# Block attention and a mixture of experts on one core: score products from plain float32 K and Q on row halves, in place of float32r parts

## The chip, the core and the metric

The kernel runs on one core of a Trainium2 chip. The metric is device time in microseconds. Three runs of the kernel before took 888.95 us in the median (888.78 to 889.32).

## What is computed

Four batches, eight heads, 576 positions, head dimension 64. Each head's scores are masked by blocks of 64 positions (a query sees its own block and all before it); the attention output becomes 2304 rows of 512, and four experts with weights per row follow.

```python
scores = scale * np.matmul(q, k.transpose(0, 1, 3, 2))
mask = block_i >= block_j                 # block_i = pos // 64
attn = softmax(np.where(mask, scores, -1e9))
x = (attn @ v).transpose(0, 2, 1, 3).reshape(2304, 512)
p = domain_probs / domain_probs.sum(-1)
out = sum(p[:, e] * (relu(x @ w1[e]) @ w2[e]) for e in range(4))
```

## The kernel before, in words

The rows are worked in five blocks (`BLOCKS`, line 21): the first holds the first 64 positions of all four batches (256 rows), the other four hold positions 64 to 575 of one batch each (512 rows). The experts' part goes over the blocks in chunks of 128 hidden columns: `mm1` (line 1106) makes 12 matmuls a chunk (three products of high and low float32r parts by four slices of the 512 inputs), `relu` splits the result again, and `mm2` (line 1148) adds into four PSUM accumulators. Blocks 0 to 2 take 96 chunks; blocks 3 and 4 are done together at the end by `both_blocks` (line 1291), from sums of their inputs that `prepare` (line 1223) makes once all attention is over.

Attention of the four 512-row blocks is made of 16 units, one for a batch and a pair of heads (`unit`, line 435). `PLAN` (line 26) puts the units of batch b in phase b + 1. A unit runs as several threads:

- `k_thread` and `q_thread` load K and Q in 32-column strips and transpose them on vector, so that the head dimension lies on partitions: kT has one head on partitions 0 to 63 and the other on 64 to 127.
- `v_thread` loads V into VN.
- `s_thread` makes the scores: the keys are cut in pieces of 128 (for 512 queries that see ever more keys, pieces of 512, 448, 320, 192 columns, and one of 64 for the odd block), and pieces of up to 512 columns share a PSUM bank. `mask` writes a large negative number where a piece covers keys that a query may not see.
- `e_thread` copies the banks to S in SBUF and takes the running maximum over pieces in cm.
- `m_thread` takes the maximum over partitions on GpSimd, then vector subtracts it and scalar takes the exponential.
- `pv_flow` (line 774) multiplies by V. In phases 2 to 4 two units go together (`mates`), and both S buffers are free only after that.

There are two ways to make the scores. Phase 1 (`plain`, line 439) takes float32 kT and qT as they are: head 0 on partitions 0 to 63 and head 1 on 64 to 127, one matmul for each head and piece (line 567), with two banks for a group of pieces, one for each head; the order of pieces and the place of the odd piece come from `pieces_beside` (line 284). It draws its banks from the two att banks and two accumulator banks that are not in use yet. Phases 2 to 4 split K and Q into a high part, which is a cast to float32r, and a low part, which is the rest: KK holds K's high part on 64 partitions and its low part on the other 64, HH holds Q's high part on both halves, LL its low part, and two matmuls over 128 partitions (lines 579 and 580) make one piece of one head. The odd piece of both heads is made together (lines 628 and 629), with the two unwanted quarters masked. Their banks are the two att banks alone.

The order of the instructions is made in the program by a planner (`Flow`, line 81). Each thread yields operations with an engine and a cost; at each step `run` (line 198) takes the one that can start first, by priority among those that are near, and puts it on its engine's queue. Units start to load when the chunk number reaches `GATES` (line 37). `late` adds distance between a matmul and its inputs in the plan: 800 ns for scores in phase 1 and 3000 ns in phases 2 to 4 (lines 46 and 47), and half of that after a bank's last use. Loads go from SP's queue.

Of the kernel before, what the change touches and what calls it, by code (L numbers as in the profile page):

```python
# [17 lines left out]
PEO = 13.5  # L18
# [230 lines left out]
def kernel(  # L249
# [78 lines left out]
    for tag, n, shape, dt in (  # L328
        ("kr", 2, [P, S], F32),
        ("qr", 1, [P, 2 * MAXW], F32),  # L330
        ("kT", 1, [P, S], F32),
        ("qT", 1, [P, 2 * MAXW], F32),
        ("KK", 2, [P, 2 * S], F32R),
        ("HH", 1, [P, 2 * MAXW], F32R),
        ("LL", 1, [P, 2 * MAXW], F32R),
        ("VN", 2, [P, (MASK_BLOCK + MAXW) // P + 1, 3, D], F32),
        ("tr", 1, [P, MAXW], F32),
        ("tc", 1, [P, MAXW // 8], F32),
        ("S", 2, [P, 2 * MAXC], F32),
        ("cm", 1, [P, 2 * MAXW], F32),  # L340
        ("mx", 1, [P, 2 * MAXW], F32),
        ("sa", 1, [P, 2 * MAXW], F32),
        ("sb", 1, [P, 2 * MAXW], F32),
        ("xs", 2, [P, MAXW], F32),
        ("rc", 1, [P, MAXW], F32),
    ):
        bufs(tag, n, shape, dt, attn)
        counts[tag] = n
# [19 lines left out]
    def late(o, by):  # L368


        o.lag = by
        return o
# [62 lines left out]
    def unit(u, ua, us, ju, pu, ph, job, dst, c):  # L435
# [5 lines left out]
        pcs, C = pieces_beside(q0, q1) if plain else pieces_of(q0, q1)  # L441
# [6 lines left out]
        def k_thread():  # L448
# [16 lines left out]
            if plain:  # L465
                st["k"] = (kT, [t], [t])
                return
            KK = yield fl.take("KK", us)
            kt, kk = kT.tile, KK.tile
            a1 = yield a_copy(kk[0:64, :q1], kt[0:64, :q1], q1, [t], [kT, KK], pr)  # L470
            l1 = yield tt(BOTH, kk[64:128, :q1], kt[0:64, :q1], kk[0:64, :q1], SUB, q1, [a1], [kT, KK], pr)
            rot = MASK_BLOCK * odd
            second = []
            for to, of, n in ((q1 + rot, 0, q1 - rot), (q1, q1 - rot, rot)):
                if n:
                    second.append((yield a_copy(kk[64:128, to:to + n], kt[64:128, of:of + n], n, [t], [kT, KK], pr)))
                    second.append((yield tt(BOTH, kk[0:64, to:to + n], kt[64:128, of:of + n], kk[64:128, to:to + n],
                                            SUB, n, second[-1:], [kT, KK], pr)))
            fl.give(kT)
            st["k"] = (KK, [a1, l1], second)  # L480

        def q_thread():
# [4 lines left out]
            for h, j in ((h, j) for h in range(2) for j in range(2 if plain else 4)):  # L487
                p0, c0 = (64 * h + 32 * j, 0) if plain else (32 * j, h * W)
                vals.append((yield dma(
                    qr.tile[p0:p0 + 32, c0:c0 + W].rearrange("c (i r) -> c i r", r=32),  # L490
                    q[b, h0 + h, q0:q1, 32 * (j % 2):32 * (j % 2) + 32].rearrange("(i c) r -> c i r", c=32),
                    W * 128, u=[qr], prio=pr, packet=128)))
            yield ("until", lambda: left_first[0] == 0 and past["w"] > 2)
            qT = yield fl.take("qT", ua)
            n = W if plain else 2 * W
            t = yield op("dve", 1.04 * n + 70, lambda _: nc.vector.transpose(out=qT.tile[:, :n], in_=qr.tile[:, :n]),
                         vals, [qr, qT], pr)
            fl.give(qr)
            if plain:
                st["q"] = (qT, t)  # L500
                return
# [4 lines left out]
            fl.give(qT)  # L506
            st["q"] = (HH, LL, a, l)

        def v_thread():
# [11 lines left out]

        def mask(r, o, m, pb):

            def fn(e):
                if e == "act":
                    nc.scalar.activation(o, ident[r:r + 64, :64], AF.Copy, bias=neg, scale=0.0)
                else:
                    nc.vector.memset(o, neg)

            return op([("act", 193.0), ("dve", 120.0)], 0, fn, [m], [pb], pr - 1.0)  # L530

        banks = []
        for h in range(2):
            cur, used = [], 0
            for pc in pcs:
                if pc[0] is None and not plain:
                    continue
# [7 lines left out]
        if plain:  # L545
            banks.sort(key=lambda x: (x[1][0][0], x[0]))
        elif odd:
            banks.append((None, [pcs[-1]]))

        def s_thread():  # L550
# [6 lines left out]
            KK, ka, kb = st["k"]  # L557
            lag = LAG_FIRST if plain else LAG
            if plain:
                qT, qv = st["q"]  # L560
                Q = [qT]
                need = lambda h: ka + [qv]
                cost = lambda w: 2 * max(107.0, 2 * w / 2.4 + 2.5)

                def product(o, h, k0, n, lo):
                    hp = slice(64 * h, 64 * h + 64)
                    nc.tensor.matmul(out=o, lhsT=KK.tile[hp, k0:k0 + n], rhs=qT.tile[hp, lo:W], start=True, stop=True)  # L567
            else:
                HH, LL, qa, ql = st["q"]
                Q = [HH, LL]  # L570
                Hv = HH.tile[:, :2 * W].rearrange("p (h w) -> p h w", h=2)
                Lv = LL.tile[:, :2 * W].rearrange("p (h w) -> p h w", h=2)
                need = lambda h: (ka + kb if h is None else kb if h else ka) + [qa, ql]
                cost = lambda w: 2 * max(85.0, w / 2.4 + PEO)

                def product(o, h, k0, n, lo):
                    at = k0 + (q1 + MASK_BLOCK * odd) * h
                    hs = h
                    nc.tensor.matmul(out=o, lhsT=KK.tile[:, at:at + n], rhs=Hv[:, hs, lo:W], start=True, stop=False)  # L579
                    nc.tensor.matmul(out=o, lhsT=KK.tile[:, at:at + n], rhs=Lv[:, hs, lo:W], start=False, stop=True)  # L580

            for h, ps_list in banks:
                if plain:

                    if h:
                        continue
                    two = []
                    for _ in range(2):
                        two.append((yield fl.take("att", None, bank_tag)))

                    def fn(_, two=two, ps_list=ps_list):
                        at = 0
                        for j, a, w, _ in ps_list:
                            for g in range(2):
                                product(two[g].tile[:, at:at + w], g, q1 - P if j is None else P * j, P, a - q0)
                            at += w

                    ws = [x[2] for x in ps_list]
                    m = yield late(op("pe", 300.0 + (2 * sum(ws) + ws[0] - sum(abs(x - y) for x, y in zip(ws, ws[1:]))) / 1.2,
                                 fn, need(0), [*two, KK] + Q, pr), lag)  # L600
                    for g in range(2):
                        done, at, spots = [m], 0, {}
                        for j, a, w, _ in ps_list:
                            r = 64 if j is None else 128 if a == P * j else None
                            if r:
                                spots.setdefault(r, []).append(at)
                            at += w
                        for r, x in spots.items():
                            o = two[g].tile[r - 64:r, x[0]:x[0] + 64]
                            if len(x) == 2:  # L610
                                o = two[g].tile[r - 64:r, x[0]:2 * x[1] - x[0]].rearrange("p (n w) -> p n w", n=2)[:, :, :64]
                            i = ident[r - 64:r, :64 * len(x)]
                            i = i.rearrange("p (n w) -> p n w", n=2) if len(x) == 2 else i
                            done.append((yield op("act", 0.833 * 64 * len(x) + 140, lambda _, o=o, i=i: nc.scalar.activation(
                                o, i, AF.Copy, bias=neg, scale=0.0), [m], [two[g]], pr)))
                        st["banks"].append((g, ps_list, two[g], done))
                    continue
                pb = yield fl.take("att", None, bank_tag)
                ps = pb.tile
                use = [pb, KK] + Q  # L620
                done = []
                if h is None:
                    lo = W - MASK_BLOCK
# [887 lines left out]
```

## Time and profile before

| | |
|---|---|
| median of three runs | 888.95 us |
| span of the profiled execution | 887.2 us |
| TensorE busy | 879.6 us, 99% |
| VectorE busy | 694.1 us, 78% |
| ScalarE busy | 464.9 us, 52% |
| GpSimd busy | 139.8 us, 16% |
| hardware DMA queue q1 | 38.5% of 16 engines |

Of the profiled execution its span is known, from its first to its last instruction; the time of a run has in addition what lies before and after. Matmuls are pipelined and their ends are modelled, so the duration of one is not its cost: the distance from one start to the next is. A float32 matmul has two records, since it is issued in two parts.

### The profile page before, as it was taken

To read this page: it belongs to the slowest core of one execution; us is meant where nothing else is said; L and a number is where in the kernel's file an instruction comes from. 1 tells how busy PE (TensorE), PEld (TensorE's weight loads), DVE (VectorE), ACT (ScalarE), POOL (GpSimd) and SP (SyncE) were. 2 spreads that over 40 slices of the span, in tenths; PEclk is the share of its full clock that TensorE was granted. 3 is DMA by queue.
4 is the path that set the end of the run, shared out by engine and by line. 5 is a ranking of instruction groups with operands and counts; after the bars stand their busy time and mean duration, and the time that the engine had idled before them with its cause. 6 is when DMAs were issued, how large, how long until landed. Compare 5 with 4: busy or idle time off the path is not lost.

```text
span 887.2 us, 12597 instructions
## 1 busy us (share of the span) xinstructions
PE 879.6 (99%) x4403; PEld 712.6 (80%) x4403; DVE 694.1 (78%) x1205; ACT 464.9 (52%) x968; POOL 139.8 (16%) x53
## 2 busy tenths in 40 slices
PE   8999999999999999999999999999999999999998
PEld 6777788878878877877878878888888888888887
DVE  6899999899898898898998789965565655666532
ACT  6796766765755664656754644544343333333220
POOL 1141100422314312412412430000000000000000
PEclk9999999999999999999999999999999999999999
DMA  7877458545455355456434222312021112110002
GB/s 170 218 182 210 131 135 200 152 140 124 97 133 128 79 133 124 127 137 158 91 92 122 83 84 84 120 48 71 24 76 40 62 47 61 48 48 24 13 1 95
DMA packets 212879, 91.18 MB, mean 103 GB/s; under 512 B 126416, under 2 KB 194256, under 8 KB 212816
## 3 DMA queue, kind: packets, MB, share of 16 engines
q1 hardware_dynamic: 211808, 89.86, 38.5%
q8 instruction: 34, 0.56, 0.3%
q10 hardware_dynamic: 1008, 0.52, 0.2%
q14 instruction: 29, 0.24, 0.1%
HBM read 85.63 MB, written 4.72 MB: 102 GB/s over the span
## 4 chain that ended last, share of the span: by engine, by line
PE 94%; DMA 2%; SPq 2%; ACT 1%; DVE 1%; issue 0%; DVEq 0%
PE acc L1171 24%; PE h L1120 24%; PE acc L1417 20%; PE h L1352 10%; PE att L1352 7%; PE att L805 5%; PE att L580 2%; SPq L380 2%; PE att L579 2%; DMA probs_n<-in_moe_domain_probs_dram 1%; DMA w2r<-in_moe_w_dram 1%; PE acc L567 0%; DMA w1r<-in_moe_w_dram 0%; PE acc L805 0%; DMA S<-in_k_dram 0%
## 5 line engine op out<-in xcount | busy, mean ns | idle before, releaser
L1120 PE MATMUL h<-xh,w1h 128*128 128x512 f32 (+1 forms) x384 | 137.0, 357 | 0.0
L1120 PE MATMUL h<-xh,w1l 128*128 128x512 f32 (+1 forms) x384 | 136.0, 354 | 0.0
L1120 PE MATMUL h<-xl,w1h 128*128 128x512 f32 (+1 forms) x384 | 135.9, 354 | 0.0
L1171 PE MATMUL acc<-w2h,hh 128*128 128x512 f32 x312 | 124.0, 398 | 0.0
L1171 PE MATMUL acc<-w2h,hl 128*128 128x512 f32 x312 | 121.8, 390 | 0.6 <-DVE hl L1140 0.6
L1171 PE MATMUL acc<-w2l,hh 128*128 128x512 f32 x312 | 121.8, 390 | 0.0
L730 POOL PARTITION_ALL_REDUCE sb<-sa x26 | 84.0, 3279 | 170.8 <-DVE tr L845 99.7
L389 ACT CAST w2h<-w2r 128x512 fp32r<-128x512 f32 x113 | 70.2, 621 | 70.6 <-PE acc L1171 57.2
L396 DVE TENSOR_TENSOR w1l<-w1r,w1h 128x512 fp32r<-128x512 f32 (+1 forms) x128 | 88.3, 692 | 3.4 <-ACT w1h L389 2.2
L751 POOL PARTITION_ALL_REDUCE mx<-cm x16 | 52.8, 3299 | 222.4 <-DVE cm L396 174.9
L396 DVE TENSOR_TENSOR w2l<-w2r,w2h 128x512 fp32r<-128x512 f32 x116 | 81.0, 699 | 5.3 <-ACT w2h L389 5.1
L1138 ACT ACTIVATE hh<-h 128x512 fp32r<-128x512 f32 (+1 forms) x94 | 49.3, 524 | 66.0 <-PE h L1120 64.9
L389 ACT CAST w1h<-w1r 128x512 fp32r<-128x512 f32 (+1 forms) x109 | 66.5, 611 | 29.1 <-DMA w1r<-in_moe_w_dram 12.4
L1120 PEld LDWEIGHTS h<-xh,w1h 128*128 128x128 f32 x384 | 72.5, 189 | 11.4 <-issue 0.9
L1120 PEld LDWEIGHTS h<-xl,w1h 128*128 128x128 f32 x384 | 72.5, 189 | 10.3
L1120 PEld LDWEIGHTS h<-xh,w1l 128*128 128x128 f32 x384 | 72.4, 189 | 10.2
L1171 PEld LDWEIGHTS acc<-w2h,hl 128*128 128x128 f32 x312 | 58.6, 188 | 13.8 <-DVE hl L1140 1.1
L1171 PEld LDWEIGHTS acc<-w2h,hh 128*128 128x128 f32 x312 | 58.7, 188 | 13.5 <-issue 1.2
L1171 PEld LDWEIGHTS acc<-w2l,hh 128*128 128x128 f32 x312 | 58.8, 188 | 9.9
L1140 DVE SCALAR_TENSOR_TENSOR hl<-h,hh 128x512 fp32r<-128x512 f32 (+1 forms) x94 | 55.4, 589 | 13.4 <-ACT hh L1138 12.9
L396 DVE TENSOR_TENSOR S<-S,mx 128x1024 f32<-128x1024 f32 (+4 forms) x80 | 59.6, 788 | 1.2 <-POOL mx L751 1.1
L707 ACT ACTIVATE S<-S 128x1024 f32<-128x1024 f32 (+4 forms) x80 | 55.4, 714 | 4.3 <-DVE S L396 4.0
(335 smaller groups left out, 1816.6 us busy)
## 6 DMA issues: line engine op xcount, KB each, us to landing
w2r<-in_moe_w_dram SPq DMA_DIRECT2D x128, 256.0 KB, 2.9
w1r<-in_moe_w_dram SPq DMA_DIRECT2D x120, 256.0 KB, 3.0
qr<-in_q_dram SPq DMA_DIRECT2D x112, 64.0 KB, 2.3
kr<-in_k_dram SPq DMA_DIRECT2D x64, 72.0 KB, 2.9
VN<-in_v_dram SPq DMA_DIRECT2D x32, 128.0 KB, 2.8
out_dram<-o SPq DMA_DIRECT2D x11, 256.0 KB, 2.6
w1rp<-in_moe_w_dram SPq DMA_DIRECT2D x8, 256.0 KB, 2.8
out_dram<-op SPq DMA_DIRECT2D x4, 256.0 KB, 2.1
```

The lines of the kernel that those rows point to most:

```text
L389: o = op(engs, 0, lambda e: nc.scalar.copy(dst, src) if e == "act" else nc.vector.tensor_copy(dst, src), r, u, prio)
L396: o = op(engs, 0, lambda e: ENG[e].tensor_tensor(out=dst, in0=a, in1=b, op=alu), r, u, prio)
L707: exps.append((yield op("act", 0.833 * 2 * w + 95, lambda _: nc.scalar.activation(sv, sv, AF.Exp, scale=scale), [t], [Sb], pr)))
L730: sums.append((yield held(2300.0, op("pool", 150 + 6.3 * W, lambda _, h=h: nc.gpsimd.partition_all_reduce(sb.tile[:, h * W:h * W + W], sa. ...
L751: lambda _: nc.gpsimd.partition_all_reduce(mx.tile[:, :2 * W], src, P, RED.max),
L805: nc.tensor.matmul(out=x.tile[64 * g:64 * g + 64, W - w:W], lhsT=lhsT, rhs=rhs, start=(i == 0), stop=(i == len(todo) - 1))
L1120: nc.tensor.matmul(out=ps[:, :n], lhsT=s.tile[:, ks], rhs=x.tile[:, kc, :n], start=(kc == 0 and m == 0), stop=(kc == KC - 1 and m == 2),)
L1138: a = yield op("act", 0.833 * n + 55, lambda _: nc.scalar.activation(hh.tile[:, :n], ps[:, :n], AF.Relu), [mm], [pb, hh], 0.0)
L1140: l = yield op("dve", 1.04 * n + 70, lambda _: nc.vector.scalar_tensor_tensor(out=hl.tile[:, :n], in0=ps[:, :n], scalar=0.0, in1=hh.tile[: ...
L1171: nc.tensor.matmul(out=acc, lhsT=s.tile[:, ts], rhs=w.tile, start=(f == 0 and m == 0), stop=(f == FC - 1 and m == 2))
L1352: nc.tensor.matmul(out=ps[:, :n], lhsT=w.tile[:, ks], rhs=x[:, kc, :n], start=(start and kc == 0 and m == 0), stop=(i in (2, 3, 4) and kc ...
L1417: nc.tensor.matmul(out=acc[:, to], lhsT=s.tile[:, ts], rhs=w.tile[:, to], start=(c == 0 and x == 0), stop=(c == 3 and x == 2), skip_group_ ...
```

## The change

All 16 units make their scores in the way of phase 1. K and Q are no longer split: KK, HH and LL are gone, kT and qT have two buffers, Q is loaded once for each head, the order of pieces is that of `pieces_beside`, and the odd piece of each head stands in a bank with others and takes the last 128 keys, of which the first 64 are masked. So VN holds the last 128 rows of V for each head, in place of 64 rows of both. The masks of a group are written by scalar, one for all pieces of a bank that need the same rows. A group takes two banks at once. The distance in the plan (`lag`), the banks that phases 2 to 4 may use and the pairing of units in `pv_flow` stay.

```diff
@@ pools
-        ("qr", 1, [P, 2 * MAXW], F32),
-        ("kT", 1, [P, S], F32),
-        ("qT", 1, [P, 2 * MAXW], F32),
-        ("KK", 2, [P, 2 * S], F32R),
-        ("HH", 1, [P, 2 * MAXW], F32R),
-        ("LL", 1, [P, 2 * MAXW], F32R),
+        ("qr", 1, [P, MAXW], F32),
+        ("kT", 2, [P, S], F32),
+        ("qT", 2, [P, MAXW], F32),
@@ unit
-        pcs, C = pieces_beside(q0, q1) if plain else pieces_of(q0, q1)
+        pcs, C = pieces_beside(q0, q1)
@@ k_thread
-            if plain:
-                st["k"] = (kT, [t], [t])
-                return
-            KK = yield fl.take("KK", us)
-            kt, kk = kT.tile, KK.tile
-            a1 = yield a_copy(kk[0:64, :q1], kt[0:64, :q1], q1, [t], [kT, KK], pr)
-            l1 = yield tt(BOTH, kk[64:128, :q1], kt[0:64, :q1], kk[0:64, :q1], SUB, q1, [a1], [kT, KK], pr)
...
+            st["k"] = (kT, [t])
@@ q_thread
-            for h, j in ((h, j) for h in range(2) for j in range(2 if plain else 4)):
-                p0, c0 = (64 * h + 32 * j, 0) if plain else (32 * j, h * W)
+            for h, j in ((h, j) for h in range(2) for j in range(2)):
+                p0 = 64 * h + 32 * j
...
-            HH = yield fl.take("HH", us)
-            LL = yield fl.take("LL", us)
-            a = yield a_copy(HH.tile[:, :2 * W], qT.tile[:, :2 * W], 2 * W, [t], [qT, HH], pr)
-            l = yield tt(BOTH, LL.tile[:, :2 * W], qT.tile[:, :2 * W], HH.tile[:, :2 * W], SUB, 2 * W, [a], [qT, HH, LL], pr)
...
+            st["q"] = (qT, t)
@@ v_thread
-                r, o, n = (slice(0, P), 2 * h, P) if plain else (slice(64 * h, 64 * h + 64), 1, MASK_BLOCK)
-                jv.append((yield dma(VJ.tile[r, at, o, :], v[b, h0 + h, q1 - n:q1], n * 256, u=[VJ], prio=pr + 0.005, packet=256)))
+                n = P
+                jv.append((yield dma(VJ.tile[:, at, 2 * h, :], v[b, h0 + h, q1 - n:q1], n * 256, u=[VJ], prio=pr + 0.005, packet=256)))
@@ s_thread
-                    nc.tensor.matmul(out=o, lhsT=KK.tile[:, at:at + n], rhs=Hv[:, hs, lo:W], start=True, stop=False)
-                    nc.tensor.matmul(out=o, lhsT=KK.tile[:, at:at + n], rhs=Lv[:, hs, lo:W], start=False, stop=True)
...
+            def product(o, h, k0, n, lo):
+                hp = slice(64 * h, 64 * h + 64)
+                nc.tensor.matmul(out=o, lhsT=KK.tile[hp, k0:k0 + n], rhs=qT.tile[hp, lo:W], start=True, stop=True)
...
+                two = []
+                for _ in range(2):
+                    two.append((yield fl.take("att", None, bank_tag)))
...
+                        for g in range(2):
+                            product(two[g].tile[:, at:at + w], g, q1 - P if j is None else P * j, P, a - q0)
...
@@ pv_flow
-                                    lhsT = VJ.tile[:, j, 2 * g, :] if j is not None else VJ.tile[:, nj, 2 * g if plain else 1, :]
+                                    lhsT = VJ.tile[:, j, 2 * g, :] if j is not None else VJ.tile[:, nj, 2 * g, :]
```

## Rows read from the trace of the kernel before

**Rows 1.** The page's first line.
```profile
span 887.2 us, 12597 instructions
```
**Rows 2.** Busy time by stretch: stretch, length, engines' busy (count), granted clock, DMA share, GB/s.
```profile
0.00:50.00 50.00, 45.96 (x401) 34.74 (x401) 39.74 (x99) 34.33 (x103) 7.11 (x13) 1.00 0.78 191
...
130.00:550.00 420.00, 420.00 (x2013) 338.06 (x2010) 375.84 (x618) 248.81 (x527) 117.36 (x36) 1.00 0.47 120
```
**Rows 3.** Waits of PE: who waited for whom, us in total, times, longest.
```profile
PE att L567 <- ACT cm L683: 1.5, 2, 0.9
...
PE acc L985 <- DVE st L978: 0.2, 1, 0.2
```
**Rows 4.** The chain that ended last: start, length, engine and line, count.
```profile
137.81 2.72 PE h L1120 x12
...
462.62 5.33 PE att L805 x40
...
525.97 5.33 PE att L805 x40
```
**Rows 5.** Timeline of PE, one unit of phase 2: start, length, instruction.
```profile
202.36 0.39 PE L579 MATMUL att<-HH,KK 128*128 128x512 f32 x1
...
203.22 0.39 PE L1120 MATMUL h<-xh,w1h 128*128 128x512 f32 x1
...
205.95 0.30 PE L579 MATMUL att<-HH,KK 128*128 128x320 f32 x1
...
206.44 0.41 PE L1171 MATMUL acc<-w2h,hh 128*128 128x512 f32 x1
206.70 0.39 PE L1171 MATMUL acc<-w2l,hh 128*128 128x512 f32 x1
...
218.11 0.22 PE L628 MATMUL att<-HH,KK 128*128 128x128 f32 x1
...
218.28 0.45 PE L1120 MATMUL h<-xh,w1h 128*128 128x512 f32 x1
218.56 0.39 PE L1120 MATMUL h<-xl,w1h 128*128 128x512 f32 x1
```
**Rows 6.** Timeline of PE in phase 1, groups of two units.
```profile
61.40 0.39 PE L1171 MATMUL acc<-w2h,hl 128*128 128x512 f32 x1
61.72 1.13 PE L567 MATMUL acc<-qT,kT 64*128 64x192 f32 x8
62.78 0.50 PE L1171 MATMUL acc<-w2h,hh 128*128 128x512 f32 x1
63.12 0.40 PE L1171 MATMUL acc<-w2l,hh 128*128 128x512 f32 x1
...
83.38 0.40 PE L1171 MATMUL acc<-w2h,hl 128*128 128x512 f32 x1
83.70 1.13 PE L567 MATMUL acc<-qT,kT 64*128 64x512 f32 x4
84.66 1.09 PE L567 MATMUL att<-qT,kT 64*128 64x448 f32 x8
85.68 0.50 PE L1171 MATMUL acc<-w2h,hh 128*128 128x512 f32 x1
```
**Rows 7.** Groups by line and form, VectorE: count, busy us, mean ns, idle before.
```profile
L396 DVE TENSOR_TENSOR LL<-qT,HH 128x1024 fp32r<-128x1024 f32 x12 | 19.0, 1580 | 0.2
...
L396 DVE TENSOR_TENSOR KK<-kT,KK 64x576 fp32r<-64x576 f32 x12 | 10.8, 897 | 1.1 <-ACT KK L389 0.7
```
**Rows 8.** The same view, ScalarE: emptying and masking of score banks.
```profile
L683 ACT COPY S<-att 128x512 f32<-128x512 f32 x56 | 32.7, 583 | 4.3 <-PE att L580 3.8
...
L526 ACT ACTIVATE att<-ident 64x64 f32<-64x64 f32 x90 | 20.0, 223 | 20.4 <-PE att L629 6.8 <-PE att L580 6.1 <-DVE probs_n L1444 1.9
```
**Rows 9.** Tile S3h: durations min/median/max, first and last start.
```profile
L1352 PE MATMUL h<-S3h,w1hp x8: 389/389/389, 555.2 to 789.1; 128*128 128x512 f32 x8
...
L396 DVE TENSOR_TENSOR S3l<-xr,S3h x1: 1217/1217/1217, 547.5 to 547.5; 128x1024 fp32r<-128x1024 f32 x1
```

More of the change, by code (lines that the diff above doesn't have):

```diff
@@ L494, in q_thread @@
             qT = yield fl.take("qT", ua)
-            n = W if plain else 2 * W
-            t = yield op("dve", 1.04 * n + 70, lambda _: nc.vector.transpose(out=qT.tile[:, :n], in_=qr.tile[:, :n]),
+            t = yield op("dve", 1.04 * W + 70, lambda _: nc.vector.transpose(out=qT.tile[:, :W], in_=qr.tile[:, :W]),
                          vals, [qr, qT], pr)
             fl.give(qr)
-            if plain:
-                st["q"] = (qT, t)
-                return
-            HH = yield fl.take("HH", us)
-            LL = yield fl.take("LL", us)
-            a = yield a_copy(HH.tile[:, :2 * W], qT.tile[:, :2 * W], 2 * W, [t], [qT, HH], pr)
-            l = yield tt(BOTH, LL.tile[:, :2 * W], qT.tile[:, :2 * W], HH.tile[:, :2 * W], SUB, 2 * W, [a], [qT, HH, LL], pr)
-            fl.give(qT)
-            st["q"] = (HH, LL, a, l)
+            st["q"] = (qT, t)
         def v_thread():
@@ L520, in v_thread @@
             st["v"] = (VJ, jv)
[L522 to L530, printed above, removed]
         banks = []
@@ L535, in unit @@
             for pc in pcs:
-                if pc[0] is None and not plain:
-                    continue
                 if used + pc[2] > 512:
@@ L544, in unit @@
                 banks.append((h, cur))
[L545 to L548, printed above, removed]
+        banks.sort(key=lambda x: (x[1][0][0], x[0]))
         def s_thread():
@@ L556, in s_thread @@
             st["banks"] = []
-            KK, ka, kb = st["k"]
+            KK, ka = st["k"]
             lag = LAG_FIRST if plain else LAG
[L559 to L578, printed above, removed]
-                    nc.tensor.matmul(out=o, lhsT=KK.tile[:, at:at + n], rhs=Hv[:, hs, lo:W], start=True, stop=False)
-                    nc.tensor.matmul(out=o, lhsT=KK.tile[:, at:at + n], rhs=Lv[:, hs, lo:W], start=False, stop=True)
@@ L582, in s_thread @@
-            for h, ps_list in banks:
[L583 to L616, printed above, removed]
-                    continue
[L618 to L623, printed above, removed]
-                    n = 2 * MASK_BLOCK
-                    def fn(_, ps=ps, n=n, lo=lo):
-                        lhsT = KK.tile[:, q1 - MASK_BLOCK:q1 + MASK_BLOCK]
-                        nc.tensor.matmul(out=ps[:, :n], lhsT=lhsT, rhs=Hv[:, :, lo:W], start=True, stop=False)
-                        nc.tensor.matmul(out=ps[:, :n], lhsT=lhsT, rhs=Lv[:, :, lo:W], start=False, stop=True)
-                    m = yield late(op("pe", 220.0, fn, need(None), use, pr), lag)
-                    m1 = yield mask(64, ps[64:128, 0:64], m, pb)
-                    m2 = yield mask(0, ps[0:64, 64:128], m, pb)
-                    done = [m, m1, m2]
-                else:
@@ new lines, in s_thread, with fn @@
+            qT, qv = st["q"]
+            def product(o, h, k0, n, lo):
+                hp = slice(64 * h, 64 * h + 64)
+                nc.tensor.matmul(out=o, lhsT=KK.tile[hp, k0:k0 + n], rhs=qT.tile[hp, lo:W], start=True, stop=True)
+            for h, ps_list in banks:
+                if h:
+                    continue
+                two = []
+                for _ in range(2):
+                    two.append((yield fl.take("att", None, bank_tag)))
+                def fn(_, two=two, ps_list=ps_list):
@@ L636, in s_thread @@
                     at = 0
-                    corners = []
                     for j, a, w, _ in ps_list:
-                        def fn(_, o=ps[:, at:at + w], j=j, h=h, a=a):
-                            product(o, h, P * j, P, a - q0)
-                        m = yield late(op("pe", cost(w), fn, need(h), use, pr), lag)
-                        done = [m]
-                        if a == P * j:
-                            corners.append(at)
-                        at += w
-                    for x in corners:
-                        done.append((yield mask(64, ps[64:128, x:x + 64], done[0], pb)))
@@ L650, in s_thread @@
-                st["banks"].append((h, ps_list, pb, done))
-            fl.give(KK, *Q)
+                        for g in range(2):
+                            product(two[g].tile[:, at:at + w], g, q1 - P if j is None else P * j, P, a - q0)
+                        at += w
+                ws = [x[2] for x in ps_list]
+                m = yield late(op("pe", 300.0 + (2 * sum(ws) + ws[0] - sum(abs(x - y) for x, y in zip(ws, ws[1:]))) / 1.2,
+                             fn, ka + [qv], [*two, KK, qT], pr), lag)
@@ new lines, in s_thread @@
+                for g in range(2):
+                    done, at, spots = [m], 0, {}
+                    for j, a, w, _ in ps_list:
+                        r = 64 if j is None else 128 if a == P * j else None
+                        if r:
+                            spots.setdefault(r, []).append(at)
+                        at += w
+                    for r, x in spots.items():
+                        o = two[g].tile[r - 64:r, x[0]:x[0] + 64]
+                        if len(x) == 2:
+                            o = two[g].tile[r - 64:r, x[0]:2 * x[1] - x[0]].rearrange("p (n w) -> p n w", n=2)[:, :, :64]
+                        i = ident[r - 64:r, :64 * len(x)]
+                        i = i.rearrange("p (n w) -> p n w", n=2) if len(x) == 2 else i
+                        done.append((yield op("act", 0.833 * 64 * len(x) + 140, lambda _, o=o, i=i: nc.scalar.activation(
+                            o, i, AF.Copy, bias=neg, scale=0.0), [m], [two[g]], pr)))
+                    st["banks"].append((g, ps_list, two[g], done))
@@ L653, in e_thread @@
+            fl.give(KK, qT)
         def e_thread():
@@ L662, in e_thread @@
                 cu = [] if alone else [cm]
-                if h is None:
-                    _, a, w, c0 = ps_list[0]
-                    pv = ps[:, :2 * w].rearrange("p (h w) -> p h w", h=2)
-                    e = yield a_copy(Sv[:, :, c0:c0 + w], pv, 2 * w, done, [pb, Sb], pr, True)
-                    st["evac"].append(e)
-                    if not alone:
-                        base = Sv[:, :, a - q0:W] if len(pcs) == 2 else cv[:, :, a - q0:W]
-                        st["evac"].append((yield tt("dve", cv[:, :, a - q0:W], pv, base, MAX, 2 * w, done + st["evac"],
-                                                    [pb, Sb] + cu, pr)))
-                else:
-                    tot = sum(x[2] for x in ps_list)
-                    c0 = ps_list[0][3]
-                    moves = [(Sv[:, h, c0:c0 + tot], ps[:, :tot])]
-                    r1 = min([x[1] for x in pcs[1:]], default=q0) - q0
-                    if r1 and ps_list[0][0] == 0:
-                        moves.append((cv[:, h, :r1], ps[:, :r1]))
-                    n = tot + r1 * (len(moves) - 1)
-                    def fn(e, moves=moves):
-                        for d_, s_ in moves:
-                            (nc.scalar.copy if e == "act" else nc.vector.tensor_copy)(d_, s_)
-                    e = yield op([("act", 0.833 * n + 60 * len(moves)), ("dve", 1.04 * n + 70 * len(moves))], 0, fn, done,
-                                 [pb, Sb] + cu, pr - (0.0 if plain else 1.0))
-                    st["evac"].append(e)
-                    at = 0
-                    for j, a, w, _ in ps_list:
-                        r = a - q0
-                        if j == 0:
-                            pass
-                        else:
-                            base = Sv[:, h, r:W] if j == 1 else cv[:, h, r:W]
-                            st["evac"].append((yield tt("dve", cv[:, h, r:W], ps[:, at:at + w], base, MAX, w,
-                                                        done + st["evac"], [pb, Sb] + cu, pr)))
-                        at += w
@@ new lines, in e_thread, with fn @@
+                tot = sum(x[2] for x in ps_list)
+                c0 = ps_list[0][3]
+                moves = [(Sv[:, h, c0:c0 + tot], ps[:, :tot])]
+                r1 = min([x[1] for x in pcs[1:]], default=q0) - q0
+                if r1 and ps_list[0][0] == 0:
+                    moves.append((cv[:, h, :r1], ps[:, :r1]))
+                n = tot + r1 * (len(moves) - 1)
+                def fn(e, moves=moves):
+                    for d_, s_ in moves:
+                        (nc.scalar.copy if e == "act" else nc.vector.tensor_copy)(d_, s_)
@@ new lines, in e_thread @@
+                e = yield op([("act", 0.833 * n + 60 * len(moves)), ("dve", 1.04 * n + 70 * len(moves))], 0, fn, done,
+                             [pb, Sb] + cu, pr - (0.0 if plain else 1.0))
+                st["evac"].append(e)
+                at = 0
+                for j, a, w, _ in ps_list:
+                    r = a - q0
+                    if j == 0:
+                        pass
+                    else:
+                        base = Sv[:, h, r:W] if j == 1 else cv[:, h, r:W]
+                        st["evac"].append((yield tt("dve", cv[:, h, r:W], ps[:, at:at + w], base, MAX, w,
+                                                    done + st["evac"], [pb, Sb] + cu, pr)))
+                    at += w
```

13 lines of the change are left out of this document (2 added, 11 removed).

## The prediction

> **What bounds the kernel now.** I read the span first [rows 1], then the busy time by stage. Between 130 and 550 us, where the twelve units that the change touches do their scores, the tensor engine is busy for 420.00 of 420 us at a granted clock of 1.00 of full speed, that is 2.4 GHz; vector is at 376 and scalar at 249 us [rows 2]. A busy tensor engine could still be slow, so I looked at the distance between starts: twelve 512-column matmuls of the first expert layer take 2.72 us, 0.227 each [rows 4], and 512 columns at 2.4 GHz are 0.213. Then the waits of the tensor engine: seven rows, 3.9 us in all, of which [rows 3] holds the first and the last, and none of it in this stage, which is busy throughout. So in the stage of the change the end is set by tensor time alone: whatever is added to its queue is added to the span, and work taken from vector and scalar has no wait left to shorten.
>
> The profiled execution spans 887.2 us [rows 1]; the median of the runs is 888.95, 1.75 more, for what lies around the span. I add the change's sum to the median and take those 1.75 us as unchanged.
>
> **Tensor work removed.** A unit now makes 18 score matmuls in six groups. By starts, one head's first two pieces (512 and 448 columns, high and low part of Q each) run from 202.36 to 203.22, 0.86 us; its last two (320 and 192) from 205.95 to 206.44, 0.49, and the matmul behind takes 0.26 where 0.227 is usual, so 0.03 more. The other head does the same. The joint last piece takes 0.17 (218.11 to 218.28), with 0.05 behind it [rows 5]. Together 2 x (0.86 + 0.49 + 0.03) + 0.17 + 0.05 = 2.98 us a unit; the other eleven units have the same starts to 0.01 us.
>
> **Tensor work added.** The new path is the one of the four units of the second block, so its price stands in this trace. In one of them a pair of 512-column products followed at once by the pairs of 448 and 64 columns runs from 83.70 to 85.68: 0.96 for the first 512 columns, 1.02 for the second 512. The 192 and 320 columns, alone, run from 61.72 to 62.78: 1.06 [rows 6]. Both heads go side by side on their row halves, and four passes of 512 columns are 4 x 512 / 2.4 GHz = 0.85 us, so the passes run at full speed. What comes on top are edges:
> - Ahead: the matmul before the group keeps its place 0.32 us instead of 0.227 (83.38 to 83.70, 61.40 to 61.72): 0.09.
> - At the start and the end of a group alone: 1.06 - 0.85 = 0.21, some 0.11 at the start (the first 512 columns need 0.96) and 0.10 at the end.
> - Behind: the next matmul takes 0.34 instead of 0.227 (62.78 to 63.12): 0.11.
>
> In the second block four spare accumulator banks let the first two groups stand together. In the later units only the two att banks are there, and a group takes both; the next group can't start before both are emptied. So there will be three separate groups a unit: 512 columns, 0.85 + 0.21 = 1.06; 448 and 64, the measured 1.02 with its own start of 0.11, 1.13; 320 and 192, 1.06. With three times 0.09 ahead and 0.11 behind that is 3.25 + 0.60 = 3.85 us. Less the 2.98 removed: 0.87 us a unit, 10.4 us for twelve. The bounds: if the first two groups did stand together, 1.98 + 1.06 + 2 x 0.20 = 3.44, so +0.46 a unit and +5.5 us in all; from above, each group might wait on its banks as in the second block, where two groups waited 1.5 us in all for a scalar copy [rows 3], that is 0.2 us for each of eight groups. Over 36 groups that would be 7 us more, +17.2. I take 10.4, since the plan asks 3 us of distance between a score group and its inputs in these units against 0.8 in the second block, and at that distance no score group waits today.
>
> **Work off the path.** On vector the low part of Q goes (12 x 1.58 = 19.0 us) and both low parts of K (0.90 us for the larger piece of a unit) [rows 7]; the Q transposes halve, and the casts to high parts leave scalar and vector. With no wait of the tensor engine behind it, I cost this gain at nothing. Four of the eight Q loads of a unit go from SP's queue, and its two short V loads double from 64 to 128 rows of 256 bytes; the DMA engines are 47% busy in this stage [rows 2], so I cost both at nothing; were the V loads late, the weighted sum of that unit would wait. The masks move from either engine to scalar alone, six a unit instead of eight, 0.22 us each [rows 8]; they lie between a group and the freeing of its banks, not on the tensor queue. The new second buffers for K and Q let a transpose start before the last unit's scores are done; nothing on the tensor engine waits for a transpose today.
>
> Should a bank still be late, what is queued behind the waiting group is every expert matmul, since the queue is in order; scalar and vector, which empty banks, don't wait on that group, so it would be a delay and no deadlock.
>
> **Sum.** 888.95 + 10.4 = 899.4 us, 1.2% slower. About 0.2% is what a measurement of this kernel can tell from no change.
>
> **Rivals.**
> Edges vanish (faster). The place is the border between a score group and the expert matmuls. Were the edges paid only in the second block, the passes alone would be 1536 x 4 / 2.4 GHz = 2.56 us a unit, 0.42 under the 2.98 removed: 12 x 0.42 = 5.0 us gained, 883.9. It decides from the point where the edges fall below 0.42 us a unit. Against it: in [rows 6] they are there at both groups, with the queue full ahead and behind, and they sum to 1.29 in three groups. For it: only that the rows come from another stage. I give 5%. The Trainium skill ("TensorEngine Tiling (Array Packing)", Theoretical Speedup) promises up to twice the rate when the contracted dimension is 64 or less, and taken without edges it gives this outcome. By that rule the trace agrees on the two halves running side by side, while its edges take more than the rule gains here.
>
> Banks emptied too slowly (much slower). Both att banks belong to one group at a time, so emptying no longer overlaps the next scores. Scores, maxima and weighted sums form a loop: two units share the buffers, and a pair of units ends with its weighted sum at 462.62, the next at 525.97, 63 us later [rows 4]. The last inputs of the final expert stage are ready at 548.7 (547.5 + 1.2) and used from 555.2 [rows 9], 6.5 us of slack; the 10.4 us of added tensor work stretch the stage and widen that to 17. So the loop may lengthen by 17 / 12 = 1.4 us a unit before the tensor engine waits. I estimate from [rows 8] that it doesn't: a round is 1.1 us of scores, two copies of 0.58 and up to four masks of 0.22 on scalar, and the 1.8 us that the plan leaves, about 5 to 6; two rounds and a last group are 11 to 13 us, where the six groups now take from 202.36 to 218.28, 16 [rows 5]. If each unit lost 3 us all the same, 36 - 17 = 19 more, 918. I give 6%. The Trainium skill (the same page, PSUM Bottleneck) warns that tiling speeds the matmuls and not the emptying of their banks, which can become the bound. In this trace the emptying costs the tensor engine 1.5 us in the second block and nothing later.
>
> Groups stand together (less slow), 888.95 + 5.5 = 894.4: it needs four free banks, and the expert sums hold the others. 2%.
>
> No effect: if a hidden stall of the tensor engine goes with the vector work and pays for the scores, 889. With 420.00 of 420 us busy there is hardly room. 2%.
>
> **How the numbers follow.** Forecast 85%, edges vanish 5%, banks 6%, groups together 2%, no effect 2%. The forecast is the likeliest. Its own sums run from 896 (edges smaller by a fifth, 12 x 0.28 us) to 904 (a wait of 0.13 us at each of 36 groups); the rivals, 15% together, lie outside, and that is the range. Faster by over 0.2%: 5%. Within: 2%. Slower: 93%.
>
> **What would show it.** Right: twelve units with three score groups each at the product's line, each about 1.06 to 1.13 us long, the matmul ahead of it at 0.32 and the one behind at 0.34; vector's busy time down by over 30 us (LL and the larger part of KK alone are 19.0 + 10.8) [rows 7]; tensor still busy for all of the stage; the start of the final expert stage some 10 us later. Wrong: score groups without edges; idle tensor time ahead of score groups put down to scalar or vector on att, or ahead of the first S3 or A22 matmul; or two groups of a unit back to back.

## The result

The changed kernel takes 898.85 us in the median of four runs (897.96 to 899.56) against 889.04 for the kernel before (888.78 to 889.32): a ratio of 1.0103, with a 95% interval from 1.009 to 1.0116. The forecast was 899.4, 1.2% slower, with a range from 896 to 904. The profiled execution of the changed kernel took 899.46 us; its span is 897.7 against 887.2 [rows 1], 10.4 us more before rounding.

The page's first lines of the changed kernel, then its waits of PE (first and last of seven rows, 3.7 us in all, as [rows 3]):

```profile
span 897.7 us, 12549 instructions
## 1 busy us (share of the span) xinstructions
PE 890.6 (99%) x4425; PEld 696.0 (78%) x4427; DVE 673.8 (75%) x1179; ACT 424.1 (47%) x874; POOL 138.5 (15%) x53
```
```profile
PE acc L1066 <- DVE hl L1035: 1.0, 1, 1.0
...
PE acc L880 <- DVE st L873: 0.2, 1, 0.2
```

Busy time by stretch (columns as in [rows 2]):

```profile
50.00:130.00 80.00, 79.96 (x510) 62.36 (x508) 74.79 (x143) 57.45 (x127) 15.10 (x5) 1.00 0.60 166
130.00:560.00 430.00, 430.00 (x2033) 321.39 (x2032) 364.08 (x601) 211.44 (x438) 116.05 (x36) 1.00 0.43 113
```

As before, the tensor engine is busy for the whole stage of the twelve units, 430.00 of 430 us, at full clock; the stage is longer, and vector and scalar have less to do in it. One unit of the third block in the tensor engine's timeline (line 521 is the product, 1015 and 1066 the expert matmuls), answering to [rows 5] and [rows 6]:

```profile
196.83 0.39 PE L1066 MATMUL acc<-w2h,hl 128*128 128x512 f32 x1
197.15 1.13 PE L521 MATMUL att<-qT,kT 64*128 64x512 f32 x4
198.21 0.50 PE L1066 MATMUL acc<-w2h,hh 128*128 128x512 f32 x1
198.55 0.39 PE L1066 MATMUL acc<-w2l,hh 128*128 128x512 f32 x1
...
201.53 0.39 PE L1015 MATMUL h<-xh,w1l 128*128 128x512 f32 x1
201.85 1.19 PE L521 MATMUL att<-qT,kT 64*128 64x448 f32 x8
202.97 0.50 PE L1015 MATMUL h<-xh,w1h 128*128 128x512 f32 x1
...
209.34 1.13 PE L521 MATMUL att<-qT,kT 64*128 64x192 f32 x8
210.40 0.50 PE L1066 MATMUL acc<-w2h,hh 128*128 128x512 f32 x1
```

By starts the three groups take 1.06, 1.12 and 1.06 us; the matmul ahead keeps its place 0.32 (196.83 to 197.15), the one behind 0.34 (198.21 to 198.55), where 0.227 is usual. With 0.09 and 0.11 for these at each group that is 3.84 us a unit, where the split way took 2.98 by [rows 5] (2.99 as the mean of its twelve units): 12 x 0.85 = 10.2 us. All twelve units have these distances to 0.01 us.

### The profile page after: what moved, and what is told of

Same layout as the page of the kernel before. It is cut to its first block, busy times and chain, and to the rows that moved or that the text cites. A ratio compares the mean times of both kernels' runs of the same rounds, so it can differ in the third digit from the quotient of the medians.

```text
span 897.7 us, 12549 instructions
## 1 busy us (share of the span) xinstructions
PE 890.6 (99%) x4425; PEld 696.0 (78%) x4427; DVE 673.8 (75%) x1179; ACT 424.1 (47%) x874; POOL 138.5 (15%) x53
## 4 chain that ended last, share of the span: by engine, by line
PE 96%; DMA 2%; SPq 1%; DVE 0%; issue 0%; ACT 0%; DVEq 0%; ACTq 0%
PE acc L1066 25%; PE h L1015 24%; PE acc L1312 19%; PE h L1247 10%; PE att L1247 7%; PE att L521 5%; PE att L700 5%; SPq L377 1%; PE acc L521 1%; DMA qr<-in_q_dram 0%; DMA probs_n<-in_moe_domain_probs_dram 0%; PE acc L700 0%; DMA w1r<-in_moe_w_dram 0%; DMA S<-in_k_dram 0%; DVE hl L1035 0%
## 5 line engine op out<-in xcount | busy, mean ns | idle before, releaser
L1015 PE MATMUL h<-xl,w1h 128*128 128x512 f32 (+1 forms) x376 | 132.8, 353 | 0.0
L1066 PE MATMUL acc<-w2h,hh 128*128 128x512 f32 x296 | 119.9, 405 | 0.0
L1066 PE MATMUL acc<-w2h,hl 128*128 128x512 f32 x296 | 115.8, 391 | 1.1 <-DVE hl L1035 1.0
L1066 PE MATMUL acc<-w2l,hh 128*128 128x512 f32 x296 | 115.8, 391 | 0.0
L386 ACT CAST w2h<-w2r 128x512 fp32r<-128x512 f32 x106 | 65.9, 622 | 73.1 <-PE acc L1066 60.3
L393 DVE TENSOR_TENSOR w2l<-w2r,w2h 128x512 fp32r<-128x512 f32 x114 | 84.4, 742 | 19.4 <-ACT w2h L386 19.0
L1066 PEld LDWEIGHTS acc<-w2h,hh 128*128 128x128 f32 x296 | 55.6, 188 | 23.5 <-issue 13.4
L1066 PEld LDWEIGHTS acc<-w2h,hl 128*128 128x128 f32 x296 | 55.6, 188 | 14.1 <-DVE hl L1035 2.2
L386 ACT CAST w1h<-w1r 128x512 fp32r<-128x512 f32 (+1 forms) x95 | 56.1, 592 | 19.2 <-PE att L1247 11.4
L1066 PEld LDWEIGHTS acc<-w2l,hh 128*128 128x128 f32 x296 | 55.8, 188 | 9.2
```

The costliest lines, as they stand in the source:

```text
L386: o = op(engs, 0, lambda e: nc.scalar.copy(dst, src) if e == "act" else nc.vector.tensor_copy(dst, src), r, u, prio)
L393: o = op(engs, 0, lambda e: ENG[e].tensor_tensor(out=dst, in0=a, in1=b, op=alu), r, u, prio)
L1015: nc.tensor.matmul(out=ps[:, :n], lhsT=s.tile[:, ks], rhs=x.tile[:, kc, :n], start=(kc == 0 and m == 0), stop=(kc == KC - 1 and m == 2),)
L1066: nc.tensor.matmul(out=acc, lhsT=s.tile[:, ts], rhs=w.tile, start=(f == 0 and m == 0), stop=(f == FC - 1 and m == 2))
```

## The experiments

Whole runs of one kernel differ by up to some 3.4 us. Two kernels were profiled twice, and their profiles differ in the first 140 us, which end at the first expert matmul of the second block (512 columns). The stretch from there to the first matmul of the final expert stage, and the final stage itself, repeat: the changed kernel, profiled in two calls, has 423.54 us twice for the one and 335.47 twice for the other. So beside the ratios of whole runs the table gives the middle stretch, by the starts of these two matmuls. In some kernels one or two score groups of the first of the twelve units come ahead of the stretch; they are added with their length and borders (1.26, 1.32 or, for three float32r products, 1.10 us), so that each row holds all groups of all twelve units.

| kernel | middle stretch | + groups ahead | sum | over the kernel before |
|---|---|---|---|---|
| before | 414.12 | none | 414.12 | |
| changed | 423.54 | 1.26 | 424.80 | 10.68 |
| one block changed | 416.39 | 1.26 | 417.65 | 3.53 |
| removed work put back | 424.84 | none | 424.84 | 10.72 |
| distance of 800 ns | 422.11 | 2.58 | 424.69 | 10.57 |
| four groups a unit | 428.82 | 1.26 | 430.08 | 15.96 |
| three float32r products | 419.40 | 1.10 | 420.50 | 6.38 |

The theory: the price is tensor time; of what a unit takes beyond its passes (3.84 - 2.56 = 1.28 us) half lies at the borders of a group with expert matmuls (0.60) and half at the group's own start and end. The rivals: it comes from the attention loop or the banks; or the tensor time rose by more and the relief of vector and scalar paid some of it back.

### One block of three (e1_one_block)

The kernel before, with the plain path for the scores of phase 2 too, and the split for phases 3 and 4; `sp` takes the place of `plain` in loads, scores and V's odd piece:

```diff
-        plain = ph == 1
...
-        pcs, C = pieces_beside(q0, q1) if plain else pieces_of(q0, q1)
+        plain, sp = ph == 1, ph <= 2
...
+        pcs, C = pieces_beside(q0, q1) if sp else pieces_of(q0, q1)
```

> The kernel before, with the scores of the third block alone (4 of the 12 units) made from plain float32 K and Q on row halves; the other 8 units keep the split. Theory (the time is tensor time, 0.85 us for each unit changed, by starts in the two traces 3.84 against 2.99): 889.0 + 4 x 0.85 = 892.4 us. Rival (the cost comes with the whole, from a longer loop of attention or from the start of the final expert stage): not linear in the units, 889 to 890 with 4 of 12.

Measured: 892.37 us, a ratio of 1.0034 (1.0022 to 1.0047); middle stretch 3.53 us longer. A third of the units costs a third of the whole (10.68 / 3 = 3.56). With four units and with twelve the price of a unit is the same (0.88 and 0.89 us), so the cost goes with the units.

### Removed work put back (e2_work_back, e8_work_back)

The changed kernel with the double Q load, the wide transpose, HH, LL and KK of the kernel before (KK with one buffer); the products read kT and qT, and are still made to wait for the parts.

```diff
-        ("qr", 1, [P, MAXW], F32),
-        ("qT", 2, [P, MAXW], F32),
+        ("qr", 1, [P, 2 * MAXW], F32),
+        ("qT", 2, [P, 2 * MAXW], F32),
+        ("KK", 1, [P, 2 * S], F32R),
+        ("HH", 1, [P, 2 * MAXW], F32R),
+        ("LL", 1, [P, 2 * MAXW], F32R),
...
+            a = yield a_copy(HH.tile[:, :2 * W], qT.tile[:, :2 * W], 2 * W, [t], [qT, HH], pr)
+            t = yield tt(BOTH, LL.tile[:, :2 * W], qT.tile[:, :2 * W], HH.tile[:, :2 * W], SUB, 2 * W, [a], [qT, HH, LL], pr)
```

> The changed kernel, with the removed work put back and its results not used: Q is loaded twice and transposed at double width, and the high and low parts of K and Q are made on vector and scalar as before; the scores still come from plain K and Q. Theory (work off the tensor engine was covered before and its removal gave nothing): as the changed kernel, 898.9 within 1 us. Rival (the relief of vector and scalar paid back a part of a larger tensor cost): slower than the changed kernel, by 2 us or more, with waits of the tensor engine on vector or scalar.

> The changed kernel with the removed work on vector and scalar put back, a second time, now beside the changed kernel on one chip. Theory (the removed work was covered): the same time as the changed kernel, within 0.1% and with the same span of some 897.7 us. Rival (the relief pays something back): 2 us over the changed kernel, as the first comparison across two calls left possible (1.0126 against 1.0103 of the kernel before, with intervals that overlap).

Measured: 900.7 us, 1.0126 (1.0111 to 1.0142), and 902.71, 1.0144 (1.0123 to 1.0165); the changed kernel beside the second took 900.07, 1.0122 (1.0105 to 1.0138). By medians that is 2.6 us more, with intervals that overlap: taken as whole runs, the second comparison gives the rival's number and not the theory's 0.1%. The busy times by stretch of the first of the two profiles:

```profile
130.00:550.00 420.00, 420.00 (x1988) 313.13 (x1989) 372.03 (x608) 236.53 (x483) 116.78 (x36) 1.00 0.47 118
```

Vector and scalar are back at 372 and 237 us, near the 376 and 249 of [rows 2], and the tensor engine is busy for 420.00 of 420 all the same. The middle stretch is 0.04 us longer than the changed kernel's. The final stage is 0.45 longer (335.92 against 335.47, in both profiles), but not on the tensor engine: from its first matmul to the start of its last one it takes 331.87 us in all four profiles. The 0.45 lies between the issue of the last output's transfer and the end of the span (2.83 us against 2.40); why is not shown.

The rest of the 2.6 lies in the first 140 us, and up to some 128 us the two kernels issue the same instructions on vector, scalar and the tensor engine (and the same loads of Q up to 122 us), so the work put back can't be its direct cause. The first of the two profiles takes less there than the changed kernel (120.21 us from the first expert matmul to the second block, against 121.55), the second more (122.51). The second has a wait of 1.2 us for a scalar copy at 49 us and, behind it, a granted clock of 0.66:

```profile
50.00:55.00 5.00, 5.00 (x20) 2.12 (x19) 4.07 (x11) 4.47 (x11) 5.00 (x2) 0.66 0.87 281
```

That is 5 x 0.34 = 1.7 us of full speed lost, an estimate; the first profile, of the same program, has 1.00 there. The granted clocks of whole runs fit: three of the four runs of the second put-back lie below 1.00 (902.39, 903.04 and 903.08 us), and the one at 1.00 took 900.22, where the changed kernel beside it took 898.70, 899.99 and 900.14 at 1.00. No run shows that the relief was worth anything in the stage of the twelve units, beyond the 0.04 us.

### Four groups a unit (e3_four_groups)

```diff
+                if ph > 1 and ps_list[0][0] == 3:
+                    m = yield late(op("pe", 700.0, lambda _, fn=fn, x=ps_list: fn(_, ps_list=x[:1]), ka + [qv], [*two, KK, qT], pr), lag)
+                    m = yield op("pe", 900.0, lambda _, fn=fn, x=ps_list: fn(_, ps_list=x[1:], at=x[0][2]), [Val(m.t + 1500.0, "pe")],
+                                 [*two, KK, qT], pr)
+                else:
+                    m = yield late(op("pe", 300.0 + (2 * sum(ws) + ws[0] - sum(abs(x - y) for x, y in zip(ws, ws[1:]))) / 1.2,
...
```

> The changed kernel, with the last score group of each of the 12 units (192 and 320 columns) cut in two groups that expert matmuls separate; the same matmuls otherwise. Theory (each border between a score group and expert matmuls costs a fixed sum, 0.20 us around the group and 0.21 inside it): 12 x 0.41 = 4.9 us more than the changed kernel, 903.8. Rival (the cost lies in the float32 passes and not in the borders): within 1 us of the changed kernel.

Measured: 905.58 us, 1.0179 (1.0165 to 1.0194). The two halves of the last group in the tensor engine's timeline:

```profile
486.79 0.39 PE L1070 MATMUL acc<-w2h,hl 128*128 128x512 f32 x1
487.11 0.60 PE L521 MATMUL att<-qT,kT 64*128 64x192 f32 x4
487.63 0.50 PE L1070 MATMUL acc<-w2h,hh 128*128 128x512 f32 x1
487.97 0.39 PE L1070 MATMUL acc<-w2l,hh 128*128 128x512 f32 x1
...
489.91 0.81 PE L521 MATMUL att<-qT,kT 64*128 64x320 f32 x4
490.65 0.50 PE L1019 MATMUL h<-xh,w1h 128*128 128x512 f32 x1
```

The same matmuls that took 1.06 us together take 0.52 + 0.74 = 1.26 apart, and a second pair of borders adds 0.20: 0.40 a unit, 4.8 in all. The middle stretch is 15.96 - 10.68 = 5.3 us longer; the half microsecond between is not traced to a line. A group's borders cost what the forecast took for them.

### Distance of 800 ns (e4_lag_800)

```diff
-LAG, LAG_PV = 3000.0, 3000.0
+LAG, LAG_PV = 800.0, 3000.0
```

> The changed kernel with the distance in the plan between a score matmul and its inputs at 800 ns in all units instead of 3000. Theory (the banks are emptied well in time and the price is tensor time at the borders): same number of groups and borders, 898.9 within 1.5 us, or up to 3 us more where a group now waits for a copy as in the second block before. Rival (emptying the two banks of a group is near its limit): over 5 us more, with waits of score groups on scalar or vector in most units.

Measured: 899.66 us, 1.0121 (1.0103 to 1.0139), against 1.0122 for the changed kernel beside it. The first of its waits, and the stage of the twelve units:

```profile
PE att L521 <- ACT cm L578: 1.9, 2, 1.6
```
```profile
130.00:550.00 420.00, 420.00 (x1990) 313.26 (x1989) 355.41 (x594) 208.66 (x432) 116.04 (x36) 1.00 0.44 113
```

Two score groups wait, for 1.9 us, both in the second block (25.85 and 48.39 us), and none between 130 and 550 us. The banks are emptied in time with 2.2 us of distance less; the rival of slow banks falls.

### Three float32r products (e5_three_r)

K and Q are split again, in the row-half layout; the product of the low parts is left out.

```diff
+            terms = [(ks[0], qs[0])] if plain else [(ks[0], qs[0]), (ks[0], qs[1]), (ks[1], qs[0])]
...
-                nc.tensor.matmul(out=o, lhsT=KK.tile[hp, k0:k0 + n], rhs=qT.tile[hp, lo:W], start=True, stop=True)
+                nc.tensor.matmul(out=o, lhsT=kx.tile[hp, k0:k0 + n], rhs=qx.tile[hp, lo:W], start=x == 0, stop=x == len(terms) - 1)
```

> The changed kernel with its row halves and its three groups a unit, but in the 12 units K and Q are split into float32r parts again, all in the row-half layout, and three float32r matmuls (high by high, high by low, low by high) take the place of one float32 matmul; the product of the two low parts is left out. 512 columns then need 3 x 512 / 2.4 GHz = 0.64 us in place of 0.85. Theory (the edges belong to the change of the array's shape and stay at 0.41 a group, whatever the type): 3 x 1.05 = 3.16 us a unit, 0.17 over the split way, so 889.0 + 2.1 = 891.1. Rival (the edges belong to float32 and its two-part issue): 1.92 us and little more a unit, 877 to 880, faster than both kernels.

Measured: 895.41 us, 1.0073 (1.0057 to 1.0088): slower than the split way, faster than float32, and neither expectation's number. A group in its timeline:

```profile
417.42 0.39 PE L1091 MATMUL acc<-w2h,hl 128*128 128x512 f32 x1
417.74 0.50 PE L545 MATMUL att<-HH,KH 64*128 64x512 f32 x2
418.07 0.40 PE L545 MATMUL att<-LL,KH 64*128 64x512 f32 x2
418.31 0.40 PE L545 MATMUL att<-HH,KL 64*128 64x512 f32 x2
418.63 0.50 PE L1091 MATMUL acc<-w2h,hh 128*128 128x512 f32 x1
418.97 0.40 PE L1091 MATMUL acc<-w2l,hh 128*128 128x512 f32 x1
```

The borders are those of float32: 0.32 ahead, 0.34 behind. So they belong to the row-half shape next to the full one and not to the type of float32. Inside, the group takes 0.89 us where the passes need 0.64, so 0.25 for start and end, near float32's 0.21; the groups with short pieces take 1.06 and 0.97 for the same 0.64 (the pieces of 64 columns are shown at the end of this text). Together 2.92 + 0.60 = 3.52 a unit, 12 x 0.53 = 6.4 over the split way, and the middle stretch is 6.38 longer. My 3.16 had left out what the short pieces cost.

### All units split (e6_split_all)

If a split unit costs 2.99 us and a plain one of the second block 3.44 to 3.84, the opposite change might beat both kernels: the kernel before with `sp = False` for all 16 units.

> The kernel before, with the split scores in the 4 units of the second block too, so that all 16 units go the way that the change removes. Theory (a split unit costs the tensor engine 2.99 us; a plain one 3.45 to 3.84): 4 x 0.5 = 2 us less than the kernel before, some 887. Rival (in the first 130 us vector is the limit, at 76 of 80 us between 50 and 130, and the split's 4 us of vector work a unit make the tensor engine wait): 889 to 893, with waits ahead of score groups.

Measured: 909.01 us, 1.0223 (1.0207 to 1.0239), much worse than either. The longest waits of the tensor engine, and two stretches:

```profile
PE h L1120 <- DVE xh L389: 3.4, 1, 3.4
PE acc L1171 <- DVE hl L1140: 3.1, 1, 3.1
PE acc L805 <- ACT w2h L389: 2.7, 1, 2.7
PE att L580 <- DVE LL L396: 2.4, 2, 1.6
```
```profile
60.00:100.00 40.00, 37.56 (x228) 31.46 (x225) 38.42 (x64) 27.66 (x61) 6.46 (x3) 0.94 0.62 163
...
145.00:200.00 55.00, 49.78 (x220) 38.76 (x219) 50.00 (x85) 33.89 (x74) 11.45 (x4) 0.91 0.54 133
```

Vector's share alone doesn't tell why: between 60 and 100 us it was as full in the kernel before (39.15 of 40), and the tensor engine waited for nothing there:

```profile
60.00:100.00 40.00, 40.00 (x256) 32.16 (x255) 39.15 (x74) 31.56 (x71) 3.22 (x1) 1.00 0.65 174
```

The order on vector tells more. The wait for hl, the low part of the hidden layer, ends at 23.44 us. In vector's queue hl stands behind the transpose of Q, which waits 2.80 us for the doubled load of Q, where it waited 0.84 in the kernel before:

```profile
21.83 1.25 DVE L496 STREAM_TRANSPOSE qT<-qr 128x1024 f32<-128x1024 f32 x1 [2.80 <-DMA qr<-in_q_dram]
23.00 0.39 DVE L1140 SCALAR_TENSOR_TENSOR hl<-h,hh 128x256 fp32r<-128x256 f32 x1
```

The waits for LL (until 45.54 and 152.91 us) are for the split's own work, and the one for x (until 157.31) follows the second of them: vector starts on the last steps to x when the split's subtractions are done. The tensor engine's idle stretches over 0.15 us sum to 17.6 us, against 3.9 in the kernel before. The granted clock also falls, to 0.94 and 0.91 of full speed as the mean of the stretches that hold such waits (0.50 from 155 to 160 us, the level of 1.2 GHz); 0.989 over the span is some 10 us of full speed lost, an estimate that partly overlaps the idle time. How much of the 20 us each took is not shown. So work whose removal gave nothing in the later blocks costs some 20 us when it is added to the four units of the second one, and none of the versions beat the kernel before.

### The changed kernel again (e7_after)

No edit; it ran beside the second put-back, the distance of 800 ns and the split of all units.

> The changed kernel as it is, on the same chip as the runs beside it. Both theories: 1.0103 of the kernel before, 1.009 to 1.012.

Measured: 900.07 us, 1.0122 (1.0105 to 1.0138), just above what was expected, with the middle stretch the same to 0.01 us.

## Why the prediction was right

**The bound.** That tensor time alone sets the end of the stage held: 430.00 of 430 us busy, and the removed work, put back, changes the stage by 0.04 us.

**The price of a unit.** Forecast 3.85 less 2.98, 0.87 us; measured 3.84 less 2.99, 0.85. Each part was within 0.01 us: 1.06, 1.13 and 1.06 forecast for the groups, 1.06, 1.12 and 1.06 measured, and the borders at 0.09 and 0.11. The prices came from units that already went the new way, in another stage; e1_one_block shows that they scale by units, and e3_four_groups that they scale by borders.

**Three separate groups.** They are separate in all twelve units. What I had not said: in the last unit of the second block the first two groups, together before [rows 6], now stand apart too, with expert matmuls between, some 0.4 us more by the price of a group's edges, an estimate. The plan of that stage leaves the old one at 49 us, where a transpose of K comes earlier on vector, as the second K buffer allows.

**The sum.** 10.4 us forecast over the median; 9.8 measured between medians, 10.4 between the two profiled spans, 10.68 in the middle stretch. Of the 10.68 the groups and their borders are 10.2; the rest is not traced to a line. The final stage is the same to 0.01 us (335.47 against 335.48), and starts 10.4 us later (562.20 against 551.76).

**The rivals.** Edges vanish: no, they are at every group. Groups together: no, three in every unit. No effect: no, the interval starts at 1.009. Banks emptied too slowly: no. A unit's scores now run from 197.15 to 210.40, 13 us, in place of 16 [rows 5]; I had estimated 11 to 13. The loop got shorter (60.4 us between the last two weighted sums, in place of 63.4), and the last weighted sum starts at 505.81 against 525.97 [rows 4], though the expert work beside it runs later:

```profile
445.43 5.33 PE att L700 x40
505.81 5.33 PE att L700 x40
```
```profile
L1247 PE MATMUL h<-S3h,w1hp x16: 388/390/390, 565.6 to 860.7; 128*128 128x512 f32 x16
...
L393 DVE TENSOR_TENSOR S3l<-xr,S3h x1: 1217/1217/1217, 528.4 to 528.4; 128x1024 fp32r<-128x1024 f32 x1
```

S3 is ready at 529.6 and used from 565.6: 36 us of slack, where there were 6.5 [rows 9]. The Trainium skill ("TensorEngine Tiling (Array Packing)", PSUM Bottleneck) says that tiling speeds up the tensor engine and not the emptying of PSUM, whose copies may become the bottleneck. No run here shows that they did, and e4_lag_800 speaks against it.

**Off the path.** I expected vector's busy time to fall by over 30 us; it fell by 20.3, from 694.1 to 673.8, and scalar's by 40.8. So that sign of being right did not come. I had missed two things. The planner puts casts on either engine by cost, and with vector relieved it gives it more of them: casts of w1 to its high part on vector rose from 19 to 29, 5.0 us (with the work put back, in e2_work_back, they are 18):

```profile
L386 DVE CAST w1h<-w1r 128x512 fp32r<-128x512 f32 x29 | 12.9, 445 | 23.6 <-PE h L1247 18.9 <-PE h L1015 4.5
```

And more of the subtractions that make the low parts of w1 and w2 run long. Most take 0.68 us; 7 of them took over 0.8 in the kernel before and 15 in the changed one, together some 9 us more, and every one of these while GpSimd takes a maximum or a sum over partitions, as here:

```profile
213.95 3.22 POOL L646 PARTITION_ALL_REDUCE mx<-cm  x1 [17.75 <-DVE cm L393]
214.11 2.28 DVE L393 TENSOR_TENSOR w2l<-w2r,w2h 128x512 fp32r<-128x512 f32 x1 [0.35 <-ACT w2h L386]
```

Both changed the row and not the time.

## What to carry to other kernels

Where an engine is full, price a change on it by distances between starts, taken from places where the new form already runs, and count the borders: here passes of equal length (2.56 us a unit either way) hide a difference of 0.85 us that is all edges. Where runs scatter by more than the effect, cut the span at two matmuls that every version has: the stretch between them repeated to 0.01 us where whole runs differed by some 3. Work on an engine off the path has its price by stage: the split of twelve units cost nothing that shows where the tensor engine was the bound, and that of four units some 20 us in the second block, where the tensor engine came to wait for it.

## What the runs showed beside that

A switch between full-height and row-half matmuls costs 0.20 us at the neighbours and some 0.21 to 0.25 inside the group, whether the products are float32 or float32r (e3_four_groups, e5_three_r). The weighted sums, matmuls of 128 by 64, have the same borders in the kernel before, 0.32 ahead and 0.33 behind:

```profile
462.23 0.39 PE L1120 MATMUL h<-xh,w1l 128*128 128x512 f32 x1
462.55 5.40 PE L805 MATMUL att<-S,VN 128*64 128x512 f32 x40
467.88 0.50 PE L1120 MATMUL h<-xh,w1h 128*128 128x512 f32 x1
468.21 0.39 PE L1120 MATMUL h<-xl,w1h 128*128 128x512 f32 x1
```

On row halves three float32r products of 64 columns for two heads take 0.35 us (402.38 to 402.73 in e5_three_r's timeline, with the end of the group) where the passes need 0.08, so short pieces are dear there:

```profile
402.38 0.19 PE L545 MATMUL att<-HH,KH 64*128 64x64 f32 x2
402.41 0.28 PE L545 MATMUL att<-LL,KH 64*128 64x64 f32 x2
402.52 0.28 PE L545 MATMUL att<-HH,KL 64*128 64x64 f32 x2
402.73 0.50 PE L1040 MATMUL h<-xh,w1h 128*128 128x512 f32 x1
```
